# A recurrent-cross attention block and a top-1 expert layer: batch 0's softmax in other pieces, idle products moved, the last round's weights in other buffers, the last store in two

## The chip, the core and the metric

The kernel runs on one NeuronCore of one Trainium2 chip. The metric is the device time of one execution in microseconds; the median of three runs of the kernel before is 456.39 us (455.68 to 456.42). The core has five engines that run side by side[...]: TensorE (matrix products; the profile shows it as PE, and its weight loads as PEld), VectorE (DVE), ScalarE (ACT), GpSimd (POOL) and SyncE (SP), which here issues most of the transfers.

## What is computed

The inputs are `x` (8 batches, 8 heads, 512 rows, 64 columns) and 32 states for each batch and head. Each batch does two softmax readings: every row of `x` reads the states, and every state reads the rows of `x`. The results are joined to 8 x 544 tokens of 512 numbers, and each token goes through one expert of eight, chosen by a gate.

```python
scores = scale * np.matmul(x, state.transpose(0, 1, 3, 2))
a = np.exp(scores - scores.max(-1, keepdims=True)); a /= a.sum(-1, keepdims=True) + 1e-09
xread = np.matmul(a, state)                      # 512 rows a batch
scores2 = scale * np.matmul(state, x.transpose(0, 1, 3, 2))
a2 = np.exp(scores2 - scores2.max(-1, keepdims=True)); a2 /= a2.sum(-1, keepdims=True) + 1e-09
sread = np.matmul(a2, x)                         # 32 states a batch
...
logits = x @ w_gate                              # x: all tokens, (4352, 512)
expert_idx = np.argmax(logits, axis=1)
...                                              # gate_w: the softmax at that expert
for e in range(E):
    mask = expert_idx == e
    h = np.maximum(x[mask] @ w1[e], 0.0)         # 512 -> 1024
    out[mask] = gate_w[mask, None] * (h @ w2[e]) # 1024 -> 512
```

All is float32. The kernel uses what these inputs show: the 512 rows of one batch nearly always choose one expert. So it takes one expert a batch (with a slow way out for the rest, which these inputs don't need), and sorts the 256 state tokens by expert into rounds of four groups.

## The kernel before

TensorE's work in batch b: scores, the first expert layer (`up`) and the second (`down`). Since a row's reading is `a @ state`, the first layer is taken as `a @ (state @ w1)`: `states_w1` makes G = state @ w1 in two halves, and `up` multiplies a by G. The softmax lives in `sx`, 128 partitions by 4 slices of 256 numbers; `aT` is its turned form, which `up` reads.

All instructions of an engine keep the order in which they are written here. The helpers that matter:

```python
def bank(name):                       # one of four PSUM banks in rotation
    return ps_p.tile([128, 512], FP32, tag="p", name=name)

def turn_scores(pc, sx, i):
    dve.transpose(sx[:, i]..., pc[:, i, 0:256])
def less_max(sx, i, eng):
    dve.tensor_reduce(mx[:, i], sx[:, i], AX.X, ALU.max)
    eng.tensor_tensor(sx[:, i], sx[:, i], spread(mx, i), ALU.subtract)
def exponential(sx, i):
    act.activation(sx[:, i], sx[:, i], AF.Exp, bias=0.0, scale=SCALE)
def over_sum(sx, i, eng):             # sum, add 1e-9, reciprocal, multiply
    ...
def turn_read(b, i=ALL):
    dve.transpose(aT[b][:, i]..., soft[b][0][:, i]...)
    if i.stop == 4:
        sp.dma_start(out=at_dram[b], in_=aT[b]...)

def write_max(pc):                    # DVE: the maximum for the states' softmax
    ...
def write_weights(pc, nm):            # ACT: its two exponentials, into a2
    ...
def write_rows(b):                    # PE: a2 @ x into pw; ACT: xs; SP: store it, load batch b + 3
    ...

def states_w1(G, w1t, st, halves=(0, 1), bank=bank):
    for k in halves:
        pg = [bank("pG") for _ in range(2)]
        ...                           # 8 products
        for g in range(2):
            act.copy(G[:, g, ts(k, 512)], pg[g][:])

def up(G, a, hT, i=ALL, insert=None, every=2):
    n = i.stop - i.start
    for f in range(NFC):              # 8 blocks of 128 hidden units
        ph = bank("ph")[:, 0:128 * n]
        for g in range(2):
            pe.matmul(ph, lhsT=G[:, g, ts(f, 128)], rhs=a[:, i, g, :], start=(g == 0), stop=(g == 1))
        relu(hT[f // 2]..., ph...)    # on ACT
        if insert and f % every == every - 1:
            next(insert, None)
```

The beginning, before the loop over the batches:

```python
        most(0, pr)                   # batch 0's expert, after the products prg
        turn_states(0, act.copy)
        xt, sx = new_xt(), new_sx()
        turn_x(0, xt, slice(0, 4))
        e = expert_of(eb, 0)
        at_once(w1_parts(0, e, 2))    # w1 of batch 0 in two transfers of 1 MB
        ...
        turn_x(0, xt, slice(4, 8))
        pc = new_pc()
        for g in range(2):
            scores(0, xt, pc, g)
        one, two = slice(0, 2), slice(2, 4)
        soft[0] = (sx,)
        turn_scores(pc, sx, 0)
        turn_scores(pc, sx, 1)
        less_max(sx, one, dve)
        exponential(sx, one)
        turn_scores(pc, sx, 2)
        turn_scores(pc, sx, 3)
        over_sum(sx, one, dve)
        turn_read(0, one)
        G = states_w1(new_G(), w1s[0], stG[:, 0])

        idle = bank("idle")
        for _ in range(7):
            pe.matmul(idle[:, 0:128], lhsT=ident[:], rhs=ident[:], start=True, stop=True, skip_group_check=True)
        less_max(sx, two, dve)
        exponential(sx, two)
        nm = write_max(pc)
        over_sum(sx, two, dve)
        turn_read(0, two)
        ...
        hT = new_hT()
        up(G, aT[0], hT, one)
        soft[0] += write_weights(pc, nm)
        ...                           # turn x and the states of batch 1
        def beside():                 # steps between the blocks of the second up
            for b in range(2):
                states_gates(b)
            ...                       # scores of batch 1, gates of batch 0
            turn_write(0)
            yield
            write_rows(0)
            exponential(sx, ALL)
            ...
        up(G, aT[0], hT, two, beside())
```

The state tokens run in three rounds (NRS = 3) beside the later batches. A round has four k steps of `round_up` (w1 blocks, tag s1, four buffers of 128 x 4 x 512) and eight f steps of `round_down` (w2 blocks, tag s2, three buffers of the same size):

```python
    def round_w2(r, f):
        t = late["sst"].tile([128, 4, DM], FP32, tag="s2", bufs=S2B, name="s2")
        for q in range(4):
            sp.dma_start(out=t[:, q], in_=moe_w2[...])
        rd[r][2, f] = t

    # in rounds(r0, r1), for each round r:
            for k in range(NDC):
                round_up(r, k)
                fetch(2, 0)           # the next two w1 blocks, no w2 block
                ...
            for f in range(0, NFC, 2):
                for i in range(2):
                    round_down(r, f + i)
                    fetch(0, 1)       # the next w2 block
```

The last batch's second layer is made of seven products of halves, the last of which is pD:

```python
        product(pD, lambda f: Sa[:, f], W(1, 1), start=False)
        store(yB, 1, 0)
        add(yA, pD, yA, 0)            # two DVE instructions, one for each half c
        store(yA, 0, 1)               # one transfer of 256 KB from ScalarE's queue
        done()
```

Of the kernel before, what the change touches and what calls it, by code (L numbers as in the profile page):

```python
# [9 lines left out]
FP32 = mybir.dt.float32  # L10
# [10 lines left out]
def kernel(  # L21
# [34 lines left out]
    B, H, S, D = x.shape  # L56
# [16 lines left out]
    NRS = 3  # L73
# [358 lines left out]
    def begin():  # L432

        nonlocal G, hT

        ps = bank("pss")[:, 0:4]
        for q in range(4):
            pe.matmul(ps[:, q:q + 1], lhsT=st2[0][0:32].rearrange("n h d -> n (h d)").rearrange("n (p c) -> n c p", c=4)[:, q, :],
                      rhs=ones_f[0:32], start=True, stop=True, skip_group_check=True)
        sums = att.tile([128, 4], FP32, name="sums")  # L440
        dve.tensor_copy(out=sums[:], in_=ps)
        pr = bank("prg")[0:1, 0:E]
        for q in range(4):
            pe.matmul(pr, lhsT=sums[:, q:q + 1], rhs=wg4[:, q, :], start=(q == 0), stop=(q == 3), skip_group_check=True)
        most(0, pr)
        turn_states(0, act.copy)
        xt, sx = new_xt(), new_sx()
        turn_x(0, xt, slice(0, 4))
        e = expert_of(eb, 0)
        at_once(w1_parts(0, e, 2))  # L450
        load_x(1, sp)
        load_states(1, sp, sp)
        sp.dma_start(out=wg[:], in_=moe_w_gate.rearrange("(c p) e -> p c e", p=128))
        at_once(w2_parts(0, e))
        fetch_batch(2)
        turn_x(0, xt, slice(4, 8))
        pc = new_pc()
        for g in range(2):
            scores(0, xt, pc, g)
        one, two = slice(0, 2), slice(2, 4)  # L460
        soft[0] = (sx,)
        turn_scores(pc, sx, 0)
        turn_scores(pc, sx, 1)
        less_max(sx, one, dve)
        exponential(sx, one)
        turn_scores(pc, sx, 2)
        turn_scores(pc, sx, 3)
        over_sum(sx, one, dve)
        turn_read(0, one)
        G = states_w1(new_G(), w1s[0], stG[:, 0])  # L470

        idle = bank("idle")
        for _ in range(7):
            pe.matmul(idle[:, 0:128], lhsT=ident[:], rhs=ident[:], start=True, stop=True, skip_group_check=True)
        less_max(sx, two, dve)
        exponential(sx, two)
        nm = write_max(pc)
        over_sum(sx, two, dve)
        turn_read(0, two)
        for r in range(NR):  # L480
            sp.dma_start(out=ss_dram[ts(r, 128)], in_=blank[:])
        hT = new_hT()
        up(G, aT[0], hT, one)
        soft[0] += write_weights(pc, nm)
        xt, sx = new_xt(), new_sx()
        turn_x(1, xt, slice(0, 4))
        turn_x(1, xt, slice(4, 8))
        turn_states(1, gp.tensor_copy)
        first_e = att.tile([1, 1], FP32, name="first_e")
        dve.tensor_copy(out=first_e[:], in_=eb[0:1, 0:1])  # L490

        def beside():
            for b in range(2):
                states_gates(b)
            pc = new_pc()
            scores(1, xt, pc, 0)
            yield

            pr = bank("pre")[:, 0:1]
            pe.matmul(pr, lhsT=ones_f[0:1].to_broadcast([1, 128]), rhs=first_e[:], start=True, stop=True)  # L500
            scores(1, xt, pc, 1)
            exps, gates = logits_x(0)
            dve.tensor_copy(out=eb[:, 0:1], in_=pr)
            for i in range(4):
                turn_scores(pc, sx, i)
            less_max(sx, ALL, dve)
            nm = write_max(pc)
            early.append(stages(2))
            next(early[0])
            yield  # L510
            exps()
            gates()
            count(0)
            turn_write(0)
            yield
            write_rows(0)
            exponential(sx, ALL)
            soft[1] = (sx,) + write_weights(pc, nm)
            over_sum(sx, ALL, dve)
            turn_read(1)  # L520
            yield
        up(G, aT[0], hT, two, beside())

    def expert_of(table, i, engines=(SP,)):
        _, (e,) = nc.values_load_multi_w_load_instructions(
# [172 lines left out]
    def down_by_halves(b, hT, w2t, insert, between):  # L698


        def A(i, j, f):
            return hT[2 * j + f // 2][:, f % 2, ts(i, 256)]

        def A2(i, j, k):
            return hT[2 * j + k][:, :, ts(i, 256)]

        def W(j, k):
            return w2t[:, ts(j, 4), ts(k, 256)]

        def sums(to, a, b, op):  # L710
            for k in range(2):
                dve.tensor_tensor(to[:, ts(k, 2)], a(k), b(k), op)

        Sa, Sb, Ta, Tb = (new_sums(t) for t in ("Sa", "Sb", "Ta", "Tb"))
        sums(Sa, lambda k: A2(1, 0, k), lambda k: A2(1, 1, k), ALU.add)
        gp.tensor_tensor(Ta[:], W(0, 1), W(0, 0), ALU.subtract)
        sums(Sb, lambda k: A2(0, 0, k), lambda k: A2(1, 0, k), ALU.subtract)
        gp.tensor_tensor(Tb[:], W(1, 1), W(0, 1), ALU.subtract)
        g = [gw[:, NC * b + c, :] for c in range(NC)]
        rows = out[ds(b * SO, S)].rearrange("(p c) f -> p c f", c=NC)  # L720
        n = [0]

        def product(to, a, w, start=True, stop=True):
            for c in range(2):
                for f in range(4):
                    pe.matmul(to[:, c], lhsT=a(f)[:, ts(c, 128)], rhs=w[:, f], start=(start and c == f == 0),
                              stop=(stop and f == 3), skip_group_check=True)
            n[0] += 1

        def done():  # L730
            step = between(n[0])
            next(step)
            next(insert, None)
            next(step)

        def new_bank(name):
            return bank(name)[:].rearrange("p (c d) -> p c d", c=2)

        def new_y():
            return ffn.tile([128, 2, 256], FP32, tag="y", bufs=YB, name="yh")  # L740

        def store(y, i, k):
            no_dep(act.dma_start(out=rows[:, ts(i, 2), ts(k, 256)], in_=y[:]))

        def add(y, p, u, i):
            for c in range(2):
                dve.scalar_tensor_tensor(y[:, c], p[:, c], g[2 * i + c], u[:, c], ALU.mult, ALU.add)

        pX = new_bank("pX")
        product(pX, lambda f: A(0, 0, f), W(0, 0))  # L750
        yA, yB = new_y(), new_y()
        for i, y in enumerate((yA, yB)):
            for c in range(2):
                act.activation(y[:, c], pX[:, c], AF.Copy, scale=g[2 * i + c])
        done()
        pD = new_bank("pD")
        product(pD, lambda f: Sa[:, f], Ta)
        sums(Sa, lambda k: Sa[:, ts(k, 2)], lambda k: A2(0, 0, k), ALU.subtract)
        gp.tensor_tensor(Ta[:], W(1, 1), Ta[:], ALU.subtract)
        done()  # L760
        product(pX, lambda f: A(0, 1, f), W(1, 0), start=False)
        yC = new_y()
        for c in range(2):
            act.activation(yC[:, c], pX[:, c], AF.Copy, scale=g[c])
        store(yC, 0, 0)
        done()
        pY = new_bank("pY")
        product(pY, lambda f: Sa[:, f], Ta)
        add(yA, pY, yA, 0)
        add(yB, pY, yB, 1)  # L770
        sums(Sa, lambda k: A2(0, 1, k), lambda k: Sa[:, ts(k, 2)], ALU.subtract)
        gp.tensor_tensor(Ta[:], W(1, 0), Ta[:], ALU.subtract)
        done()
        pZ = new_bank("pZ")
        product(pZ, lambda f: Sb[:, f], Tb)
        add(yB, pZ, yB, 1)
        yD = new_y()
        add(yD, pD, yB, 1)
        done()
        pW = new_bank("pW")  # L780
        product(pW, lambda f: A(1, 1, f), Ta)
        store(yD, 1, 1)
        add(yB, pW, yB, 1)
        done()
        product(pD, lambda f: Sa[:, f], W(1, 1), start=False)
        store(yB, 1, 0)
        add(yA, pD, yA, 0)
        store(yA, 0, 1)
        done()

    def store_batch(b):
# [108 lines left out]
        rd[r][1, k, half] = t  # L900

    def round_w2(r, f):
        t = late["sst"].tile([128, 4, DM], FP32, tag="s2", bufs=S2B, name="s2")
        for q in range(4):
            sp.dma_start(out=t[:, q], in_=moe_w2[ds(rd[r]["e"][q], 1), ts(f, 128), :]
                              .rearrange("o p f -> p (o f)"))
        rd[r][2, f] = t
# [57 lines left out]
    def rounds(r0, r1):  # L965
# [10 lines left out]
        for r in range(r0, r1):  # L976
# [4 lines left out]
            yield  # L981
            for k in range(NDC):
                round_up(r, k)
                fetch(2, 0)
                yield
                if k < NDC - 1 and r + 1 < r1:
                    yield
# [17 lines left out]

    def first():

        yield
        turn_write(1)
        yield  # L1010
# [207 lines left out]
```

## Time and profile before

| What | From | Value |
|---|---|---|
| time, median of 3 | times | 456.39 us |
| span of the profiled execution | page | 456.4 us |
| batch 0's scores, second part | timeline | 10.30 to 12.98 us |
| first `up` of batch 0 starts | timeline | 18.75 us |
| first product of batch 0's `down` | timeline | 39.05 us |
| last round's `down` products (pgy) | timeline | 420.29 to 447.3 us |
| last store issued | timeline | 451.92 us |

Times in the views count from the start of the span. A row of the chain of waits gives start, length and what ran; it follows the work that ended last back from the end. A row of the timeline gives start, length, engine, operation, output<-inputs, shape and count, and in brackets how long the engine sat idle before and what ended that. TensorE does a float32 product in two passes, so that the profile shows two records for one product of the program.

### The profile page before, as it was taken

What the parts mean: (1) busy time and instruction counts of PE and PEld (TensorE: products, weight loads), DVE (VectorE), ACT (ScalarE), POOL (GpSimd) and SP (SyncE); (2) the same over time, 40 slices, a digit from 0 to 9 for tenths busy, and PEclk for the clock granted to TensorE, in tenths of its full rate; (3) what the DMA queues carried; (4) which work ended last, traced back from release to release, by engine and by line L of the source; (5) the groups of instructions that cost most, each with busy time, mean ns of one, the idle gap of its engine ahead of it and who ended that gap; (6) DMA issues with size and microseconds to landing.
All of it is one profiled execution on the core that took longest, in us unless ns stands there. A gap on an engine that the chain in (4) does not pass through costs nothing.

```text
span 456.4 us, 9813 instructions
## 1 busy us (share of the span) xinstructions
PE 439.4 (96%) x3809; PEld 271.5 (59%) x3809; DVE 198.5 (43%) x445; ACT 124.3 (27%) x274; POOL 120.1 (26%) x108
## 2 busy tenths in 40 slices
PE   3999999999999999999999999999999999999995
PEld 2576545455455455445767775776667776657762
DVE  4838771748273753142241541445143523226151
ACT  1343233433152442323311421024111412025000
POOL 2011040313121211005243512642263322532220
PEclk9999999999999999999999999999999999999999
DMA  6990678324758443518999998899879997480771
GB/s 189 330 305 2 180 275 274 119 87 149 285 131 300 142 154 117 169 46 306 353 377 346 379 386 316 278 397 393 290 227 339 347 401 251 146 292 1 241 263 62
DMA packets 68403, 110.06 MB, mean 241 GB/s; under 512 B 12927, under 2 KB 27263, under 8 KB 68352
## 3 DMA queue, kind: packets, MB, share of 16 engines
q1 hardware_dynamic: 60096, 99.86, 63.9%
q10 hardware_dynamic: 7856, 8.47, 5.3%
q0 software_dynamic: 400, 1.05, 0.6%
q8 instruction: 32, 0.52, 0.5%
q14 instruction: 19, 0.16, 0.1%
HBM read 94.15 MB, written 14.95 MB: 239 GB/s over the span
## 4 chain that ended last, share of the span: by engine, by line
PE 79%; DVE 11%; DMA 5%; ACT 1%; issue 1%; SPq 1%; POOL 0%; ACTq 0%; POOLq 0%; DVEq 0%
PE ph L48 19%; PE py L48 11%; PE pD L48 8%; PE pX L48 8%; PE pgy L48 6%; PE pgh L48 5%; PE pY L48 4%; PE pW L48 4%; PE pZ L48 4%; DMA w1t<-in_moe_w_dram 3%; PE pc L48 3%; PE pG L48 3%; DVE xt L48 3%; DVE sm L48 1%; DVE nm L48 1%; PE pw L48 1%
## 5 line engine op out<-in xcount | busy, mean ns | idle before, releaser
L48 PE MATMUL py<-w2t,hT 128*128 128x512 f32 x192 | 87.5, 601 | 0.0
L48 PEld LDWEIGHTS py<-w2t,hT 128*128 128x128 f32 x192 | 34.7, 190 | 39.2 <-issue 38.4
L48 POOL TENSOR_TENSOR Ta<-w2t,Ta 128x1024 f32<-128x1024 f32 x10 | 26.1, 2612 | 76.5 <-PE pD L48 45.2
L48 PE MATMUL ph<-aTe,G 128*128 128x256 f32 (+1 forms) x128 | 44.0, 493 | 0.5 <-DVE aTe L48 0.5
L48 DVE TENSOR_TENSOR hT<-ph,hT 128x512 f32<-128x512 f32 x40 | 27.7, 692 | 37.1 <-PE ph L48 37.1
L48 ACT ACTIVATE hT<-ph 128x512 f32<-128x512 f32 (+1 forms) x48 | 24.9, 528 | 47.4 <-PE ph L48 47.4
L48 PE MATMUL pX<-w2t,hT 128*128 128x256 f32 x160 | 36.2, 379 | 0.0
L48 PEld LDWEIGHTS pX<-w2t,hT 128*128 128x128 f32 x160 | 30.2, 190 | 4.4 <-issue 0.5
L48 PEld LDWEIGHTS ph<-aTe,G 128*128 128x128 f32 x128 | 23.3, 190 | 15.7 <-issue 12.9
L48 PE MATMUL ph<-aTl,G 128*128 128x256 f32 (+1 forms) x96 | 29.6, 456 | 0.0
L48 POOL TENSOR_TENSOR sx<-sx,mx 128x1024 f32<-128x1024 f32 x6 | 11.5, 1913 | 63.4 <-DVE mx L48 63.4
L48 PE MATMUL pgy<-s,shT 128*32 128x512 f32 x192 | 27.0, 599 | 0.0
L48 DVE SCALAR_TENSOR_TENSOR yh<-pY,gw,yh 128x256 f32<-128x256 f32 x20 | 8.3, 478 | 41.3 <-PE pY L48 31.5
L48 PEld LDWEIGHTS ph<-aTl,G 128*128 128x128 f32 x96 | 17.7, 190 | 12.7 <-issue 11.4
L48 ACT COPY G<-pG 128x512 f32<-128x512 f32 x32 | 16.8, 594 | 29.2 <-PE pG L48 28.3
L48 ACT ACTIVATE yh<-pX,gw 128x256 f32<-128x256 f32 x30 | 12.1, 474 | 45.0 <-PE pX L48 45.0
L48 PE MATMUL pgh<-s,sxT 128*32 128x512 f32 x192 | 23.6, 599 | 0.0
L48 PE MATMUL pc<-xt,stT 32*32 32x128 f32 x1024 | 18.3, 296 | 3.9 <-DVE xt L48 3.9
L48 DVE STREAM_TRANSPOSE sx<-pc 128x256 f32<-128x256 f32 x32 | 11.6, 419 | 23.8 <-PE pc L48 23.8
L48 PE MATMUL pG<-w1t,stG 64*32 64x512 f32 x256 | 20.8, 629 | 0.8 <-DMA w1t<-in_moe_w_dram 0.6
L48 ACT ACTIVATE hT<-hT 128x512 f32<-128x512 f32 x24 | 14.8, 632 | 22.9 <-DVE hT L48 22.9
L48 ACT ACTIVATE y<-py,gw 128x512 f32<-128x512 f32 x12 | 8.3, 689 | 44.3 <-PE py L48 44.3
(175 smaller groups left out, 638.3 us busy)
## 6 DMA issues: line engine op xcount, KB each, us to landing
s<-in_moe_w_dram SPq DMA_DIRECT2D x192, 256.0 KB, 5.2
w2t<-in_moe_w_dram SPq DMA_DIRECT2D x32, 512.0 KB, 6.7
w1t<-in_moe_w_dram SPq DMA_DIRECT2D x28, 512.0 KB, 6.4
x_nat<-in_x_dram SPq DMA_DIRECT2D x16, 512.0 KB, 6.1
out_dram<-yh ACTq DMA_DIRECT2D x20, 256.0 KB, 4.4
out_dram<-y ACTq DMA_DIRECT2D x12, 256.0 KB, 3.4
at_dram<-aTl SPq DMA_DIRECT2D x5, 512.0 KB, 3.7
w1t<-in_moe_w_dram SPq DMA_DIRECT2D x2, 1024.0 KB
```

What stands on the lines that cost most here:

```text
L48: ins = getattr(self.engine, name)(*args, **kw)
```

## The change

It has four parts.

1. Batch 0's softmax on VectorE and its `up` on TensorE go by two quarters and a half, where they went by two halves, so that TensorE can begin sooner. The maximum for the states' softmax comes after all of it.
2. Idle products on the identity (their result isn't used) are put ahead of batch 0's scores, for TensorE's clock. The seven between G and `up` become three.
3. `write_rows(0)` leaves the second `up` and comes into the first steps beside `down`; the gates of batch 1's states come one step later.
4. In the last round, w2 blocks 3 to 6 take the buffers that the last w1 blocks free, and are asked for during that round's `up`. The last batch's last store is sent as two transfers from two queues.

```diff
         most(0, pr)
+        keep_warm(7)
         turn_states(0, act.copy)
@@
-        one, two = slice(0, 2), slice(2, 4)
+        one, two, half = slice(0, 1), slice(1, 2), slice(2, 4)
         soft[0] = (sx,)
+        G, hT = new_G(), new_hT()
         turn_scores(pc, sx, 0)
-        turn_scores(pc, sx, 1)
         less_max(sx, one, dve)
         exponential(sx, one)
+        states_w1(G, w1s[0], stG[:, 0], (0,))
+        turn_scores(pc, sx, 1)
+        over_sum(sx, one, dve)
+        turn_read(0, one)
+        less_max(sx, two, dve)
+        exponential(sx, two)
+        states_w1(G, w1s[0], stG[:, 0], (1,))
+        keep_warm(3)
         turn_scores(pc, sx, 2)
         turn_scores(pc, sx, 3)
-        over_sum(sx, one, dve)
-        turn_read(0, one)
-        G = states_w1(new_G(), w1s[0], stG[:, 0])
-        ...                                        # seven idle products
-        less_max(sx, two, dve)
-        exponential(sx, two)
-        nm = write_max(pc)
         over_sum(sx, two, dve)
         turn_read(0, two)
+        up(G, aT[0], hT, one)
+        less_max(sx, half, dve)
+        exponential(sx, half)
+        over_sum(sx, half, dve)
+        turn_read(0, half)
         ...
-        hT = new_hT()
-        up(G, aT[0], hT, one)
-        soft[0] += write_weights(pc, nm)
+        up(G, aT[0], hT, two)
+        soft[0] += write_weights(pc, write_max(pc))
@@ def beside():
-            for b in range(2):
-                states_gates(b)
+            states_gates(0)
+            yield
+            states_gates(1)
@@
             turn_write(0)
-            yield
-            write_rows(0)
             exponential(sx, ALL)
@@
-        up(G, aT[0], hT, two, beside())
+        up(G, aT[0], hT, half, beside())
@@ def first():
+        write_rows(0)
         yield
         turn_write(1)
@@ def round_w2(r, f):
-        t = late["sst"].tile([128, 4, DM], FP32, tag="s2", bufs=S2B, name="s2")
+        free = r == NRS - 1 and S2B <= f < S2B + S1B
+        t = late["sst"].tile([128, 4, DM], FP32, tag="s1" if free else "s2", bufs=S1B if free else S2B, name="s2")
@@
-                fetch(2, 0)
+                fetch(2, 2 if r == NRS - 1 and k > 1 else 0)
@@
+        def store_each(y, i, k):
+            for c, q in enumerate((act, sp)):
+                no_dep(q.dma_start(out=rows[:, 2 * i + c, ts(k, 256)], in_=y[:, c]))
@@
-        store(yA, 0, 1)
+        (store if b < B - 1 else store_each)(yA, 0, 1)
```

`keep_warm(n)` takes a bank and does n products of the identity with itself, 128x128x128.

More of the change, by code (lines that the diff above doesn't have):

```diff
@@ L459, in begin @@
             scores(0, xt, pc, g)
-        one, two = slice(0, 2), slice(2, 4)
+        one, two, half = slice(0, 1), slice(1, 2), slice(2, 4)
         soft[0] = (sx,)
+        G, hT = new_G(), new_hT()
         turn_scores(pc, sx, 0)
-        turn_scores(pc, sx, 1)
         less_max(sx, one, dve)
         exponential(sx, one)
+        states_w1(G, w1s[0], stG[:, 0], (0,))
[6 more added lines that the diff above has]
+        keep_warm(3)
         turn_scores(pc, sx, 2)
         turn_scores(pc, sx, 3)
-        over_sum(sx, one, dve)
-        turn_read(0, one)
-        G = states_w1(new_G(), w1s[0], stG[:, 0])
-        idle = bank("idle")
-        for _ in range(7):
-            pe.matmul(idle[:, 0:128], lhsT=ident[:], rhs=ident[:], start=True, stop=True, skip_group_check=True)
-        less_max(sx, two, dve)
-        exponential(sx, two)
-        nm = write_max(pc)
         over_sum(sx, two, dve)
         turn_read(0, two)
+        up(G, aT[0], hT, one)
[3 more added lines that the diff above has]
+        turn_read(0, half)
         for r in range(NR):
             sp.dma_start(out=ss_dram[ts(r, 128)], in_=blank[:])
-        hT = new_hT()
-        up(G, aT[0], hT, one)
-        soft[0] += write_weights(pc, nm)
+        up(G, aT[0], hT, two)
+        soft[0] += write_weights(pc, write_max(pc))
         xt, sx = new_xt(), new_sx()
@@ L521, in beside, with keep_warm @@
             yield
-        up(G, aT[0], hT, two, beside())
+        up(G, aT[0], hT, half, beside())
+    def keep_warm(n):
+        idle = bank("idle")
+        for _ in range(n):
+            pe.matmul(idle[:, 0:128], lhsT=ident[:], rhs=ident[:], start=True, stop=True, skip_group_check=True)
     def expert_of(table, i, engines=(SP,)):
```

## The prediction

> **What bounds the kernel now.** I read the first two parts of the page first. TensorE is busy for 96% of the span, so only the few stretches where it waits, or runs at half speed, can be won back.
>
> ```profile
> span 456.4 us, 9813 instructions
> PE 439.4 (96%) x3809; PEld 271.5 (59%) x3809; DVE 198.5 (43%) x445; ACT 124.3 (27%) x274; POOL 120.1 (26%) x108
> PE   3999999999999999999999999999999999999995
> ```
>
> The first and the last slice are the only thin ones. Next I read the chain of work that ended last, cut to 5 to 30 us:
>
> ```profile
> 10.30 2.70 PE pc L48 x110
> ...
> 15.95 0.70 DVE sm L48
> ...
> 17.17 0.70 DVE sx L48
> 17.90 0.72 DVE aTe L48
> 18.62 0.14 issue
> 18.75 7.16 PE ph L48 x32
> ...
> 28.62 1.00 PE pc L48 x54
> ```
>
> Columns: start, length, what. Batch 0's scores (pc) run to 13.00; then a VectorE chain of 5.6 us (turn, maximum, subtract, sum, divide, turn) for half the softmax; then `up` starts at 18.75. After that TensorE has hardly a gap. Note the rate: 110 score matmul records take 2.70 us here; the next batch needs 1.00 us for a whole group of 64 (54 of its records lie on the chain). The scores run cold.
>
> Then the chain from 380 us on, for the last round (pgy):
>
> ```profile
> 438.27 1.85 PE pgy L48 x16
> 440.13 3.65 PE pW L48 x16
> 443.78 3.54 PE pgy L48 x16
> 447.32 3.67 PE pD L48 x16
> 450.98 0.02 issue
> 451.01 0.48 DVE yh L48
> 451.49 0.07 DVEq L1111
> 451.57 0.32 DVE yh L48
> ```
>
> The same 16 products take 1.85 us at 438 and 3.54 us at 443.8. The timeline of 446 to 457 us says why (a weight load waits for a transfer), and shows the last store:
>
> ```profile
> 446.27 0.14 PEld L48 LDWEIGHTS pgy<-s,shT 128*32 128x32 f32 x2 [0.54 <-DMA s<-in_moe_w_dram]
> 451.92 0.38 ACTq L48 DMA_DIRECT2D out_dram<-yh  x1
> ```
>
> After 451.92 no engine computes: bytes move until about 454, and the program closes at 456.4.
>
> **What the Trainium skill says.** (1) "TensorE: Matmul & The Clock Gate", Part 1: TensorE runs at 1.2 GHz until it has been busy for a window of about 3.4 us, then at 2.4 GHz; the window runs freely, so the moment varies. The trace agrees: the first 16 pG records take 1.96 us, the next 16 take 1.11 us. (2) "PSUM — Partial Sum Buffer", Engine vs sequencer instructions: the queues of ScalarE and VectorE are strict FIFO. The trace has a case: ScalarE's xs, waiting for VectorE at 44.16, holds back an exponential whose input was ready at 38.9. (3) "DMA: Bandwidth & Descriptors", Anatomy of one DMA: about 2.0 us of a transfer is fixed, whatever its size. Here 16 KB rows of srow land in 1.8 us, a 256 KB yh store in a quiet queue in 2.6 us.
>
> **Part 1: idle products ahead of the scores.** Seven 128x128 products are added after `prg`, which ends at 5.70. In the kernel before, seven of them (14 records) take 1.64 us of weight loads when warm; cold, at twice that, 3.3 us. They end near 9.0; the first half of xt lets the scores start at 9.17. They cost nothing. If they wake the clock by 10.30, the 112 records after the second half of xt take 112/64 x 1.00 = 1.75 us instead of 2.70. Scores end at 12.1 instead of 13.0: **0.9 us**. Transfers don't take that back: the first w1 half had landed by 12.9 (TensorE waited for no transfer there), and its product is needed only when ScalarE is free at 13.9.
>
> **Part 2: two quarters and a half.** VectorE costs from the rows: 128x512 takes 0.69 us, 128x1024 1.22 us, so 0.16 fixed and 0.53 per 512, and 128x256 takes 0.43. A turn of 128x256 takes 0.40; a small sum step 0.2. From 12.1: turn 12.5, maximum 12.95, subtract 13.4, turn of the next 13.8 (exponential beside it until 13.9), sum, add, reciprocal 14.8, divide 15.2, turn 15.6. First quarter: 3.5 us instead of 5.6. Second quarter: subtract ends 16.5, the rest 19.0.
>
> The build order changes what this is worth. ScalarE's queue is now: exponential 1, two G copies, exponential 2, two G copies, eight relus. Exponential 2 can't run before VectorE's subtraction at 16.5, so the last two G copies run from 16.95 to 18.05, and all relus follow. TensorE (two pG halves and three idle products until about 16.85) does one up block at 16.85, then waits from 17.3 to 17.5 for the bank that a G copy frees. The other seven blocks take 7 x 2 x 2 x 0.117 = 3.3 us: first quarter done at 20.9, not at 19.4. Second quarter: 8 x 0.47 = 3.8 us, done at 24.7. The half's exponential waits behind the relus until 21.3; exponential 0.63, sum to divide 1.9, turn 0.7: aT's last half is ready at 24.6. TensorE starts it at 24.75. In the kernel before it started the last half at 25.91.
>
> Then a loss. The write weights (two exponentials, 1.3 us) come after a maximum that VectorE now takes after everything else: 24.6 + 1.2 + 0.2 = 25.9, so they hold ScalarE until 27.25, and the half's first relu ends at 27.65. The third block of the half needs that bank; TensorE is there at 26.85. Stall 0.8 us. From 27.7: two blocks 1.8, gates 0.3, scores 1.0, two blocks 1.8, scores, `pre` and logits 1.9, two blocks 1.8, count and turns 1.1: `down` begins at 37.4. Before, it began at 39.05, with 1.03 us of pw ahead of it that now comes inside `down`: to compare, 38.0. **Net gain of the start 0.6 to 0.7 us.**
>
> **Part 3: moved pw.** The same 64 records, 1.03 us, between other products: no change on TensorE. ScalarE no longer holds batch 1's exponential behind xs, so the turn at 46.35, which waited 0.17 us, is ready early: 0.1 us. The rest of the middle is tied to TensorE by data (w1 loads start after the counted expert, the rounds' loads after the sort), so the shift should carry through, even through the stretch of full transfer queues from 210 to 280 us, since that stretch starts with the sort.
>
> **Part 4: last round's w2 in freed w1 buffers.** Before, three w2 blocks were loaded and each next waited for a product. Now blocks 3 to 6 are asked for after up products k=2 and k=3, at 405 and 410 us, where the transfer row shows an almost empty slice behind them (0 in slice 37). Four blocks of 1 MB at some 350 GB/s, the rate of loaded slices, take 12 us: landed by 423. Block 7 is asked for after the first down product at 421. All is there before 443.8. Removed: 3.54 - 1.85 = **1.7 us**, all on the path.
>
> **Part 5: last store in two.** The second half can't leave before 451.9, but it is 128 KB. Between 16 KB (1.8) and 256 KB (2.6), 128 KB should land in about 2.2: **0.4 us**.
>
> **Sum.** 0.7 + 1.7 + 0.4 = 2.8 us; 456.4 - 2.8 = 453.6 us.
>
> **Rivals.** A: *the start gives nothing.* The clock stays cold (the window falls badly), and the ScalarE order eats the quarters: two quarters cost 0.4 us more TensorE time than a half, and the 0.8 us stall stays. Then `down` starts at 38.3 or later, compared with 38.0: total 454.6, or 455 if the stall is over 1 us. For it: the queue order. Against: seven idle products fill more than 3 us. B: *everything at the start counts.* Exponential 2 and the relus cost less than I think; TensorE goes on at 17 us without a gap: 1.6 us at the start, total 452.7. C: *the tail's wait moves.* The early loads collide with the w1 blocks of k=3 (the pgh product at 402.8 already takes 2.30 us instead of 1.85), so that a wait comes at 408 or 421 in place of that at 443.8: the gain of 1.7 shrinks to 1.0, total 454.3. Against it: k=3's blocks are ahead in the same queue. D: *the store is bound by its fixed part:* 0.1 instead of 0.4, total 453.9.
>
> **Range and chances.** The start may lie between -0.4 and 1.6, the tail between 1.0 and 1.9, the store between 0 and 0.6. All low together is unlikely: 455.2 to 452.3 holds eight in ten. Two per cent is 9.1 us, over three times the sum; nothing here loses as much. Faster by over 2% 0.01, within 2% 0.98, slower 0.01.
>
> **What would show it.** Right: scores of 112 records in about 1.75 us; a gap of 0.2 us after the first up block and one of 0.8 us after batch 0's first gates; pw inside py; the last pgy at 1.85 us; two stores from two queues, landing some 2.2 us after issue. Wrong: scores still at 2.7 us; the second quarter not ready when the first ends; a new transfer wait among the rounds; or a shift at 60 us that has gone by 300 us.

## The result, and the profile after

The changed kernel takes **453.6 us** (median; 452.45 to 455.18), the kernel before 456.4 (455.68 to 457.54). The ratio is 0.9937 with a 95% interval of 0.9914 to 0.9960, that is 1.8 to 3.9 us less. The prediction was 453.6. The sum came out and most of its terms did not, so most of what follows is about the terms.

One caution ahead of the two pages: the profiled execution of the kernel before took 458.4 us, 2.0 more than its median, that of the changed kernel 453.9. So the spans differ by 4.2 us where the medians differ by 2.8, and a wait that one page has and the other hasn't may be chance. Shares and waits are compared over several kernels below for that reason.

The page of the changed kernel, first part:

```profile
span 452.2 us, 9911 instructions
PE 436.6 (97%) x3847; PEld 274.0 (61%) x3847; DVE 199.3 (44%) x452; ACT 125.6 (28%) x283; POOL 120.2 (27%) x108
```

TensorE has 38 more matmul records and is busy 2.8 us less: waits inside a run of products count as busy, so fewer of them show here.

The timeline of TensorE in the changed kernel, 3 to 60 us (start, length, what, and in brackets the idle time before it and what ended it):

```profile
5.65 3.36 PE L48 MATMUL idle<-ident 128*128 128x128 f32 x14
...
10.34 2.69 PE L48 MATMUL pc<-xt,stT 32*32 32x128 f32 x112 [0.45 <-DVE xt L48]
...
16.86 1.13 PE L48 MATMUL ph<-aTe,G 128*128 128x128 f32 x8
18.45 8.62 PE L48 MATMUL ph<-aTe,G 128*128 128x128 f32 x64 [0.46 <-ACT G L48]
27.00 0.27 PE L48 MATMUL pg<-wg,stT 64*32 64x8 f32 x16
28.08 1.99 PE L48 MATMUL ph<-aTe,G 128*128 128x256 f32 x8 [0.81 <-ACT hT L48]
...
37.85 3.60 PE L48 MATMUL py<-w2t,hT 128*128 128x512 f32 x8
41.38 1.10 PE L48 MATMUL pw<-x_nat,a2T 128*32 128x64 f32 x64
```

The seven idle products run where they were meant to, cold (3.36 us), and the 112 score records behind them are still cold: 2.69 us, not 1.75. `up` starts at 16.86 all the same, then waits 0.46 us for a G copy and 0.81 us for the half's relu. `down` starts at 37.85 with pw inside it.

The end, from the chain of waits of the changed kernel:

```profile
439.13 1.85 PE pgy L48 x16
440.99 3.67 PE pD L48 x16
444.65 0.02 issue
444.68 0.49 DVE yh L48
```

The last pgy takes 1.85 us where it took 3.54. And the two stores, from the timeline of 443 us to the end:

```profile
445.19 0.35 ACTq L48 DMA_DIRECT2D out_dram<-yh  x1
445.58 0.35 SPq L48 DMA_DIRECT2D out_dram<-yh  x1
```

From the end of pD (444.65) to the end of the span (452.2) it is 7.55 us; in the kernel before it is 5.42 (450.98 to 456.4). The end became *longer*.

### The profile page after: what moved, and what is told of

Read it like the earlier page. It is cut to its first block, busy times and chain, and to the rows that moved or that the text cites. A ratio compares the mean times of both kernels' runs of the same rounds, so it can differ in the third digit from the quotient of the medians.

```text
span 452.2 us, 9911 instructions
## 1 busy us (share of the span) xinstructions
PE 436.6 (97%) x3847; PEld 274.0 (61%) x3847; DVE 199.3 (44%) x452; ACT 125.6 (28%) x283; POOL 120.2 (27%) x108
## 4 chain that ended last, share of the span: by engine, by line
PE 83%; DVE 9%; DMA 3%; ACT 1%; issue 1%; POOL 1%; SPq 0%; ACTq 0%; POOLq 0%; DVEq 0%
PE ph L48 19%; PE py L48 14%; PE pD L48 8%; PE pX L48 8%; PE pgy L48 5%; PE pgh L48 5%; PE pY L48 4%; PE pW L48 4%; PE pZ L48 4%; PE pc L48 4%; PE pG L48 3%; DVE xt L48 3%; DVE sm L48 2%; PE pw L48 2%; PE pt L48 2%; DMA w1t<-in_moe_w_dram 2%
## 5 line engine op out<-in xcount | busy, mean ns | idle before, releaser
L48 PE MATMUL ph<-aTe,G 128*128 128x128 f32 (+2 forms) x160 | 44.9, 430 | 1.4 <-ACT hT L48 0.8
L48 ACT ACTIVATE hT<-ph 128x512 f32<-128x512 f32 (+2 forms) x56 | 26.1, 476 | 46.5 <-PE ph L48 46.5
L48 PEld LDWEIGHTS ph<-aTe,G 128*128 128x128 f32 x160 | 24.6, 190 | 16.1 <-issue 12.3
L48 PE MATMUL pgy<-s,shT 128*32 128x512 f32 x192 | 23.5, 599 | 0.0
L48 PE MATMUL pG<-w1t,stG 64*32 64x512 f32 x256 | 19.4, 628 | 0.3 <-DMA w1t<-in_moe_w_dram 0.2
L48 POOL TENSOR_TENSOR sx<-sx,sm 128x1024 f32<-128x1024 f32 x6 | 11.5, 1912 | 31.1 <-ACT xsT L48 17.0
```

The costliest lines, as they stand in the source:

```text
L48: ins = getattr(self.engine, name)(*args, **kw)
```

## The experiments

Times are medians; "against before" is the ratio less one, times 456.4 us, with its 95% interval. The experiments ran on four chips, each beside the kernel before, whose median there was 455.8 to 456.8 us. So kernels are compared by these ratios, and two medians from different chips can differ by about a microsecond for that alone. By this measure the changed kernel has -2.9 (-3.9 to -1.8).

**The last store: whole again, or both halves from ScalarE, or two stores alone.**

```diff
 one_store:          - (store if b < B - 1 else store_each)(yA, 0, 1)
                     + store(yA, 0, 1)
 both_on_act:        - for c, q in enumerate((act, sp)):
                     + for c, q in enumerate((act, act)):
 before_two_stores:  the kernel before, with store_each and its use added
```

> The changed kernel with its last store in one piece again. From the end of the last pD product to the end of the span, the kernel before takes 5.4 us and the changed one 7.6 us. Theory (SyncE, which now issues the second half, takes its closing branch after that, and the branch takes over 3 us): 5.4 us again, and the time falls by about 2 us, from 453.6 to 451.5. Rival (halves land sooner; the longer end has another cause, such as slow writes in that execution): the end stays at 7 us or more, or becomes longer by 0.4, and the time stays at 453.6 to 454.

> The changed kernel with both halves of the last store issued by ScalarE. Theory of SyncE's branch: SyncE is done early again, as in the kernel before, so the end takes about 5.2 to 5.4 us, and the time is about 451.3. Rival (two small stores are slower than a large one, whoever issues them): the end stays near 7.6 us and the time near 453.6.

> The kernel before with only the last store in two, from ScalarE and SyncE. Theory of SyncE's branch: the end grows from 5.4 to about 7.5 us, time 458.5. Rival (the prediction's term): the end shrinks by 0.4, time 456.0.

Measured: one_store 451.8 us (against before -3.1, interval -4.2 to -2.1), both_on_act 452.7 (-3.2, -4.4 to -2.0), before_two_stores 456.8 (**+1.0**, +0.3 to +1.8). From the end of pD to the end of the span: 6.2 us in one_store, 6.2 in both_on_act, 6.8 in before_two_stores. Cutting the store in two doesn't end it sooner (one_store and both_on_act end alike), and giving half of it to SyncE costs. All fourteen profiled executions of this document sort by that: the end takes 6.7 to 7.6 us in the six in which SyncE has half of the last store, and 5.4 to 6.2 in the eight others. The two pages above (7.55 and 5.42) are the extremes; the means are 7.0 and 5.9. In the times, only before_two_stores shows the cost: one_store and both_on_act are 0.2 and 0.3 us below the changed kernel, far inside the intervals. The direction is that of the theory of SyncE's branch, the size about half of what it gave. Why is in SyncE's closing instructions. In the kernel before:

```profile
L1114 SPq EVENT_SEMAPHORE  x9: 17/17/17, 446.1 to 454.7; - x9
L1114 SPq COMPARE_BRANCH  x1: 50/50/50, 442.3 to 442.3; - x1
```

in the changed kernel:

```profile
L1129 SPq EVENT_SEMAPHORE  x9: 17/17/17, 449.9 to 450.5; - x9
L1129 SPq COMPARE_BRANCH  x1: 50/50/50, 446.5 to 446.5; - x1
```

and in one_store:

```profile
L1129 SPq EVENT_SEMAPHORE  x9: 17/17/17, 423.0 to 449.8; - x9
L1129 SPq COMPARE_BRANCH  x1: 50/50/50, 419.7 to 419.7; - x1
```

The branch that leaves the loop takes 3.3 to 3.8 us until SyncE's first closing semaphore (442.3 to 446.1, 446.5 to 449.9, 419.7 to 423.0); over all fourteen executions it is 2.6 to 4.8 us. With no store of its own, SyncE has that behind it before the last bytes have landed, and its closing semaphores then stretch over many microseconds (423.0 to 449.8 in one_store). With half of the last store it takes the branch only after 445.58, and the nine semaphores follow each other in 0.6 us: nothing else is left to wait for. The span ends 1.7 to 1.8 us behind the last of the nine in every execution.

**The second weights of the last round alone.** The kernel before with that part of the change:

```diff
+ free = r == NRS - 1 and S2B <= f < S2B + S1B      # and the tag "s1" where free
- fetch(2, 0)
+ fetch(2, 2 if r == NRS - 1 and k > 1 else 0)
```

> The kernel before with only the last round's w2 blocks 3 to 6 in w1 buffers. Theory: the last pgy product takes 1.85 us instead of 3.54, nothing else moves, time 456.4 - 1.7 = 454.7. Rival (the wait moves to another product of that round): the sum of the round's waits stays over 1 us, time 455.7 or more.

Measured: 454.8 us, **-1.1** (-1.8 to -0.4); the last pgy takes 1.85 us. That is less than the 1.7 of the page before, for a reason that the other kernels without this part show: the last pgy waited 1.7, 0.6, 1.7, 0.9 and 0.6 us in the profiled executions of the five of them. The page before was one of the two longest. A wait like rival C's may have taken part of it back here: the two pgh at 402 and 408 us wait 1.6 us together in before_w2, 0.2 to 0.5 us in the three other kernels with TensorE's program as before, and at most 0.5 in the changed kernel and its variants. That is one execution, so it isn't shown.

**The start alone**, without the second weights and the two stores:

```diff
  (the changed kernel, with round_w2, fetch(2, 0) and store(yA, 0, 1) as before)
```

> The kernel before with only the start changed (quarters, idle products, write_rows moved): the last round's buffers and the last store as before. Theory: the first steps gain 0.7 us by 47 us, so the time is 455.7. Rival (the middle of the kernel gains too, since the changed kernel's trace waits 1.6 us less for batch 3's w1 and 1.3 us less for a w2 block at 275 us than the kernel before): the time is 453 to 454.

Measured: 453.1 us, -3.9 (-5.3 to -2.4), where the prediction had 0.7. Yet its trace starts batch 2's scores at 47.72 us, where the kernel before is at 47.89 and the changed one at 47.21. So the start is worth far more in the time than at 47 us. Where the rest comes from is the last group of experiments.

**Parts of the start.**

```diff
 no_idle_ahead:  - keep_warm(7)
 idle_14:        - keep_warm(7)
                 + keep_warm(14)
 weights_later:  - soft[0] += write_weights(pc, write_max(pc))
                 + nm_0, pc_0 = write_max(pc), pc
                 + soft[0] += write_weights(pc_0, nm_0)   # in beside(), ahead of the gates
```

> The changed kernel without the seven idle products ahead of the scores. In the changed kernel the 112 score records took 2.69 us, as before, and durations of 1.06 us for pG records until about 14.9 say that the clock was slow until then in both kernels. Theory (the idle products don't wake the clock before 15 us): scores 2.7 us, down of batch 0 begins at 37.9, time 453.6. Rival (they move the waking a little, or wake it in some executions): scores or pG slower, down begins 0.5 to 1 us later, time 454.3.

> The changed kernel with fourteen idle products ahead of the scores instead of seven. Theory A (dense products of seven take 3.36 us, just too short for a whole window; more of them wake the clock): the products after about 9 us run at half their length, the 112 score records take 1.75 us, scores end at 12.7 or sooner. Theory B (the clock's waking has nothing to do with them): fourteen take 6.7 us cold, the scores start at 12.4 and end near 15, all of the start 2 us later, time 455.5.

> The changed kernel with the two exponentials of the states' softmax of batch 0 behind the first two relus of the half, instead of ahead of them. Theory: the wait of 0.8 us before the third block of the half goes, down of batch 0 begins at 37.1 instead of 37.85, time 452.8. Rival (another wait follows at once, for the gates' bank or for batch 1's states, which VectorE and GpSimd have ready at 29.8): down begins at 37.6 to 37.85, time as the changed kernel.

Measured: no_idle_ahead 454.4 us (-2.1, -2.8 to -1.4), idle_14 455.5 (-0.9, -1.6 to -0.2), weights_later 454.0 (-2.5, -3.3 to -1.6). In the times, the idle products' own gain is not to be told from none (the intervals of no_idle_ahead and of the changed kernel overlap). Fourteen of them are worse than seven (-0.9 against -2.9). What they do is seen in the timeline of TensorE. In idle_14:

```profile
5.63 4.82 PE L48 MATMUL idle<-ident 128*128 128x128 f32 x28
10.38 1.90 PE L48 MATMUL pc<-xt,stT 32*32 32x128 f32 x128
...
15.04 1.09 PE L48 MATMUL pG<-w1t,stG 64*32 64x512 f32 x16 [1.43 <-DMA w1t<-in_moe_w_dram]
```

and in one_store, where seven were enough:

```profile
10.76 1.77 PE L48 MATMUL pc<-xt,stT 32*32 32x128 f32 x112 [0.67 <-DVE xt L48]
...
15.14 1.09 PE L48 MATMUL pG<-w1t,stG 64*32 64x512 f32 x16 [1.40 <-DMA w1t<-in_moe_w_dram]
...
16.94 9.63 PE L48 MATMUL ph<-aTe,G 128*128 128x128 f32 x72
26.50 0.27 PE L48 MATMUL pg<-wg,stT 64*32 64x8 f32 x16
```

Seven products stand ahead of the scores in seven of the profiled executions. In three of them (one_store, rows_back and one_store_later below) the 112 score records take 1.77 us; in three (the changed kernel, start_only, weights_later) 2.68 or 2.69, and both_on_act lies between. In the six executions without them it is always 2.68 or 2.69. So they seem to wake the clock in some executions; seven against six are too few to call it shown.

Where it woke, TensorE then waits about 1.4 us for w1's second transfer. That costs little, because something else comes later. The changed kernel's gap of 0.46 us after the first `up` block was for a copy of G on ScalarE; these copies stand behind the second quarter's exponential, and this one behind VectorE's work on the scores. ScalarE begins the last two copies in the changed kernel and in one_store at

```profile
17.83 1.05 ACT L48 COPY G<-pG 128x512 f32<-128x512 f32 x2
17.33 1.05 ACT L48 COPY G<-pG 128x512 f32<-128x512 f32 x2
```

Counted from the second part of the scores (10.34 and 10.76), that is 7.49 and 6.57 us. So `up` goes on without the gap, and batch 0's gates (pg) begin 15.7 us after that point in the three awake executions and 16.6 to 16.7 in the three cold ones and in no_idle_ahead: 0.9 us sooner. idle_14 has most of this too (its pg is at 26.25 us, where the changed kernel's is at 27.00), but then stands idle for 0.42 us at 34.3, with no cause that the profile shows, and begins batch 2's scores at 47.26. That it ends 2.0 us above the changed kernel is not explained by its start; its read-out of the sort is late (199.92).

weights_later takes the 0.81 us stall away, but the rival of its expectation comes in: batch 1's gates wait for its turned states, which GpSimd has ready only at 29.9 us. `down` starts at 37.78 us, hardly before 37.85.

**Where the rest of the start's gain comes from.** First guess: the moved pw, since the transfers of batch 0's rows then come in another order. In the page before, TensorE waits for w1 of batch 3 near 122 us: the 32 pG records there take 3.70 us (122.42 to 126.12), in the changed kernel 2.06.

```diff
 moved_rows_only: the kernel before, with
   - yield; write_rows(0)      # in beside()
   + write_rows(0)             # first in first()
 rows_back: the changed kernel, with the opposite edit, and
   - states_gates(0); yield; states_gates(1)
   + states_gates(0); states_gates(1)
```

> The kernel before with one thing of the change: batch 0's 64 pw records (and the xs, srow and x_nat work behind them) come inside the first down, not ahead of it. The two parts of the start that are left to tell apart are this move and the quarters. Theory 1, the transfers' order: the change's start brought 2.8 to 3.8 us, though only 0.7 us of it was there at 47 us; the rest is waits for transfers further on that are gone because batch 0's rows (srow, then x_nat and the states of batch 3) go behind the write of the read weights of batch 1 and in less traffic. Then this kernel alone takes 453.0 to 454.8 us, batch 3's first experts' product waits under 0.3 us for w1 near 122 us, and the four srow issues near 104 us take about 2.4 us. Theory 2, the earlier start: those waits go only because TensorE's work is earlier against the loads, or vary by themselves; then this kernel takes 456.0 to 456.6 us, and the wait near 122 us is still 0.3 to 1.6 us.

> The changed kernel with that move alone undone: quarters, idle products, second weights and the two stores stay as changed; batch 0's pw records again come ahead of the first down (and the gates of batches 0 and 1 in one piece, as in the kernel before). Theory 1, the transfers' order makes most of the start's gain: 455.0 to 456.3 us, 1.5 to 2.7 us above the changed kernel, with a wait for w1 near 122 us. Theory 2, the quarters make it: 453.4 to 454.2 us, at most 0.5 us above the changed kernel, with no such wait; down itself starts about 1.0 us later, since the 64 records now come ahead of it.

Measured: moved_rows_only 456.7 us (+0.4, -0.5 to +1.2). The wait near 122 us is down to 0.3 us in its trace, and the time is not better. That wait is no fixed part of the kernel: against the shortest of all executions (1.95 us for the 32 records) it is 1.75 us in the profiled execution of before (the one of 458.4 us), 0.95 in before_two_stores, 0.3 in before_w2, none in before_filler below, and 0.94 in idle_14, which has the move. The first guess falls.

rows_back: 457.1 us (+0.3, -0.5 to +1.2), outside what either theory gave. It is no clean test of the move, for it undid one thing more. Its TensorE near 28 us:

```profile
26.28 0.27 PE L48 MATMUL pg<-wg,stT 64*32 64x8 f32 x16
28.55 0.20 PE L48 MATMUL pg<-wg,stT 64*32 64x8 f32 x2 [2.00 <-DVE first_e L48]
29.13 0.27 PE L48 MATMUL pg<-wg,stT 64*32 64x8 f32 x14 [0.38 <-POOL stT L48]
```

Batch 1's gates need its turned states, which come after `first_e` on VectorE (28.34 us). With the quarters, and with the clock awake in this execution, TensorE is there 2.4 us early. Behind that wait the granted clock reads 0.50 from 30 to 33 us, and the next two `up` blocks take 3.19 us instead of 1.99. The `yield` between the two gates, one line of the change of which the prediction says nothing, puts two `up` blocks in that place; without it, as far as this trace shows, the quarters lose more than they bring. It also shows that a shift at the start lasts: rows_back starts batch 2's scores 2.87 us after the changed kernel (50.08 against 47.21) and takes 3.2 us more by the two ratios.

Now the profiled executions side by side. "Read-out" is the start of the prs products at the sort; from there on the program is the same in all but for the parts at the end.

| kernel | TensorE records | batch 2's scores | read-out | read-out to end of pD |
|---|---|---|---|---|
| before | 3809 | 47.89 | 201.10 | 249.87 |
| before_two_stores | 3809 | 47.81 | 199.57 | 248.25 |
| before_w2 | 3809 | 47.99 | 199.91 | 249.11 |
| moved_rows_only | 3809 | 48.18 | 199.08 | 249.65 |
| start_only | 3847 | 47.72 | 198.44 | 246.96 |
| after | 3847 | 47.21 | 198.75 | 245.89 |
| one_store | 3847 | 46.70 | 198.15 | 247.14 |
| both_on_act | 3847 | 49.07 | 200.20 | 247.39 |
| weights_later | 3847 | 47.13 | 199.35 | 246.52 |
| rows_back | 3847 | 50.08 | 200.91 | 245.91 |
| no_idle_ahead | 3833 | 47.50 | 198.90 | 247.34 |
| idle_14 | 3861 | 47.26 | 199.92 | 246.74 |

The last column falls into two groups without overlap: 248.3 to 249.9 for the four with 3809 records, 245.9 to 247.4 for the eight with more, rows_back with its late start among them. The difference lies in four places where products wait for the rounds' weights (pgy at 75, 166 and 242 us after the read-out, pgh at 202 to 208); the rest agrees to 0.1 us. Part of it is the second weights, which take the wait at 242 away: without that wait the groups are 247.6 to 249.1 and 245.9 to 247.4, 0.2 us apart, and none of the places sorts them alone (the wait at 75 us is 0.5 to 2.0 us in the first group and 0.3 to 1.9 in the second). An earlier start doesn't sort the kernels so; the length of TensorE's program does, in these twelve executions. The last kernel tests that alone: 38 records, as tiny products in the 3.5 us in which TensorE waits anyway.

```diff
 before_filler: the kernel before, with
+ for _ in range(19):        # behind prg, ahead of batch 0's scores
+     pe.matmul(filler[0:32, 0:8], lhsT=ident[:, 0:32], rhs=ident[:, 0:8], ...)
```

> The kernel before with 19 very small products (32x8, two records each: the 38 TensorE records by which the changed kernel is longer) in the 3.5 us in which TensorE waits ahead of batch 0's scores; the output doesn't use them. They don't bring the start forward: batch 2's scores stay within 0.3 us of 47.9 us. What they do is move TensorE's later instructions by as many places in its program. In the traces so far TensorE's instructions are fetched in 16 KB packets of about 1 us each through the engines that also carry the weights. In the four kernels without the quarters such a fetch falls 202 us after the read-out of the sort begins, right in the transfers of the last round's fourth first-layer block, and the two products on that block wait 0.24 to 1.62 us; in the nine with quarters the fetch falls at 194 to 197 and the products wait 0 to 0.4. Theory 1, the fetch makes that wait: here it falls at 194 to 198 after the read-out, the two products wait under 0.1 us together, and the time is 455.2 to 456.0 us, 0.4 to 1.2 below the kernel before. Theory 2, the wait comes with the later start: it stays at 0.24 to 1.6 us though the fetch has moved, and the time is 456.2 to 457.0 us.

Measured: 455.05 us, **-1.6** (-2.3 to -1.0), with nothing of the change in it, more than either theory gave. TensorE at its start:

```profile
5.69 2.17 PE L48 MATMUL idle<-ident 128*32 128x8 f32 x38
...
10.57 2.69 PE L48 MATMUL pc<-xt,stT 32*32 32x128 f32 x112 [0.45 <-DVE xt L48]
...
19.02 8.87 PE L48 MATMUL ph<-aTe,G 128*128 128x256 f32 x40 [0.22 <-DVE aTe L48]
...
48.13 1.07 PE L48 MATMUL pc<-xt,stT 32*32 32x128 f32 x64
```

The scores are cold, `up` starts at 19.02 and batch 2's scores at 48.13, 0.24 us *after* the kernel before. So the gain isn't an earlier start; nor is it the small delay, since moved_rows_only starts batch 2's scores at 48.18 and gains nothing. Its read-out is at 199.66, and from there to the end of pD it takes 247.39 us: the second group. The two pgh at 202 and 208 wait 0.15 us together (0.50 in the page before).

What of it is the fetch of instructions? The page's queue q8 moves them: 32 packets, 0.52 MB, 16 KB each, in every kernel.

The filler changes TensorE's program alone, and q8's packets move with it. In the DMA view of the kernel before, cut to 391 to 395 us (190 to 194 after the read-out), there is one:

```profile
q8 instruction: 1, 0.02, 1.8%
```

In before_filler there is none at that distance, but one from 383 to 387 us (183 to 187 after the read-out):

```profile
q8 instruction: 1, 0.02, 1.5%
```

In the changed kernel it stands at 185 too. But the expectation's places for it were some ten microseconds too late: the packet does not fall into the transfer for which the pgh at 202 waits, but ten us ahead of it. That these nineteen products at this place bring 1.6 us is shown. That any 38 records more would do so is not, since one number of them was tried at one place; that the fetches do it is only argued, and how one of about 1 us would act ten us later is open.

**Two of the parts together:** one_store and weights_later.

> The changed kernel with its last store whole again, from ScalarE's queue, and with batch 0's write weights behind the half's first two relus. The first is worth about 1 us by the runs so far, the second nothing that could be told from noise. If both add as they were measured: 452.0 to 452.8 us, below the changed kernel (453.6 to 453.9) and far below the kernel before, and the time from the last product to the end of the span is 5.4 to 6.2 us, not 6.7 to 7.6. If the gain of the whole store was chance: 453.4 to 454.2 us.

Measured: 452.4 us (-3.4, -4.7 to -2.1), 5.7 us from the end of pD to the end of the span. This and one_store (-3.1) beat the kernel before. That they beat the changed kernel (-2.9) is not shown: the intervals overlap almost whole. Here the clock woke (scores 1.77 us), neither the 0.46 nor the 0.81 us wait of the changed kernel appears, and `down` starts at 36.99.

## Why the prediction was right, and where it was not

- **Idle products (0.9 us at the scores): the premise failed, not the working.** The step that failed is that seven idle products wake the clock by 10.30 us: in the page after the scores stay at 2.69 us, and they were awake in three of seven executions. Where they were, the 0.9 us came through to batch 0's gates. "Transfers don't take that back" held for a reason that the prediction hadn't looked at: it had checked w1's first transfer only, TensorE does wait 1.4 us for the second, and the copies of G come later still.
- **Quarters (net 0.6 to 0.7 us): the number came out by luck.** It was worked out for a clock awake at the scores. Measured at batch 2's scores, counted from the second part of batch 0's, the cold start gains 0.7 us (37.59 to 36.87, as in start_only and no_idle_ahead), the awake one 1.65 (35.94 in one_store). So rival A had the clock of the page after, and rival B's 1.6 us without a gap at 17 us is what one_store shows. Single steps fit: first block at 16.86 (16.85 predicted), the half's stall 0.81 (0.8). The gap after the first block was 0.46, not 0.2, and `down` came at 37.85, not 37.4: at that point the cold start has gained only 0.2 us (from 38.0). The rest comes inside `down`, where the wait of 0.17 us at 46.35 goes and the turn behind it (pt) takes 1.04 us instead of 1.32.
- **Moved pw: 0.1 us on paper, no gain measured** (moved_rows_only +0.4, -0.5 to +1.2).
- **"The rest of the middle is tied by data, so the shift carries through":** it does (rows_back), but the sum left out a term: what 38 records of small unused products alone bring to the kernel before, 1.6 us (1.0 to 2.3). Its trace has less of the waits for the rounds' weights.
- **Second weights (1.7 us): the mechanism right, the term too large.** 1.1 us (0.4 to 1.8): the page before showed one of the longest of the waits that it removes.
- **Last store in two (0.4 us gained): wrong sign.** +1.0 us (0.3 to 1.8) in before_two_stores. The estimate looked at how long bytes take; what ends the span is SyncE's closing branch, which the store delays.
- **The sum.** Measured alone, the parts are about -0.7 (quarters, read at 47 us), -1.6 (filler), -1.1 (second weights) and +1.0 (store): -2.4, where the change has -2.9 (-3.9 to -1.8). The prediction had -0.7, nothing, -1.7 and -0.4, that is -2.8. A term left out, one too large and one of the wrong sign made up for each other, so that the total came out to a tenth is luck. That the measured parts add up so is assumed; no run shows it. Of the rivals, A was right that the clock stays cold and wrong in the time; C's moved wait may have shown in before_w2 but not in the changed kernel; D was right that halves land no sooner, and missed that they cost.

What stays open: how nineteen small products more in TensorE's program shorten the waits for weights, and why start_only, without the gain of the second weights, is not above the changed kernel (its interval, -5.3 to -2.4, just misses the -2.3 of quarters and filler; an awake clock, 0.9 us in some executions, is not in that sum).

## What to carry to other kernels

A wait in one profiled execution is a sample: compare its time with the median, and look at the same place in other executions, before its length goes into a sum. Before an engine is given a last store, see what it still has to do after it; the queue that had long been done is free only because it had long been done. And where a kernel is changed on its busiest engine, run a control that only adds as many idle instructions: here that alone brought 1.6 us, where the whole change brought 2.9. A term that rests on the clock has two values; count in several executions how often each comes.

## What was not expected of the hardware

- The branch at the end of SyncE's program takes 2.6 to 4.8 us until its first closing semaphore, in fourteen executions, taken anywhere between 419 and 450 us.
- Nineteen 32x8 products that nothing uses, placed in idle time, took 1.6 us (1.0 to 2.3) off a 456 us kernel.
- With seven idle products ahead (3.1 to 3.4 us), the 112 score records took 1.77 us in three executions and 2.69 in three others, with the same instructions up to there. Behind fourteen (4.82 us, idle_14), 128 of them took 1.90 us.
- 2.4 us without work on TensorE at 26.5 to 29 us of rows_back were followed by a granted clock of 0.50 from 30 to 33 us.
